# Wide loads for the first three pairs: four tokens a partition, half the heads in each half of the partitions

## The chip, the cores and the metric

The kernel runs on one core of a Trainium2 chip. The metric is the device time of one execution in microseconds (us). Engines are called PE (TensorE, with PEld for its weight loads), DVE (VectorE), ACT (ScalarE), POOL (GpSimd) and SP (SyncE, which here only issues DMAs).

## What is computed

A gated linear attention runs over B = 4 batches, H = 8 heads, S = 768 tokens, D = 48 elements a head. Its output, all heads of a token side by side, goes through a two-layer network with the gate h·cos(h):

```python
for t in range(S):
    state = alpha[:, :, t, :, None] * state + np.einsum('bhd,bhe->bhde', k[:, :, t], v[:, :, t])
    y[:, :, t] = np.einsum('bhd,bhde->bhe', q[:, :, t], state)
x = y.transpose(0, 2, 1, 3).reshape(B * S, H * D)     # [3072, 384]
h = x @ w_in                                          # [3072, 2048]
out = (h * np.cos(h)) @ w_out                         # [3072, 384]
```

alpha, q, k, v lie in DRAM as [4, 8, 768, 48] in fp32, so one token of one head is a run of 192 bytes, and neighbouring tokens of a head are neighbours in memory.

## The kernel before

**Tiling.** The tokens are cut into 12 *pairs* J of 256 tokens, three pairs a batch; each pair has two *chunks* c of 128 tokens, and the state is carried from chunk to chunk. In SBUF a partition holds two neighbouring tokens (e = 0, 1) of all eight heads, so that partitions 0 to 63 are chunk 0 and partitions 64 to 127 chunk 1. `load` (L107 to L121) fills such a tile of 384 KB by one DMA on SP's queue, in runs of two tokens (384 bytes). L110 is that DMA. All loads of a, k, q and v go through SP; W1 (`load_w1`, four pieces u) and W2 (four pieces) are issued by POOL and cast from fp32 to bf16 on the way (L125 to L135).

**One pair** goes through these steps, each a function of its own:

- `ln` (L144, ACT): logarithm of alpha into `lna`. `cums0`/`cums` (L191, L173): cumulative sums of the logarithms over the tokens of a chunk, as matmuls with triangular matrices `tri` and `strict` (L168); pairs 0 to 2 get a sum for each of their two tokens this way, later pairs multiply the two alphas first (`mul_a`, L152, POOL) and subtract (`sub`, L197, DVE). `icp` and `exps` (L206, L213, ACT): exp of minus and of plus that sum; `session` does the four of a later pair and the next pair's `ln`.
- `scale_k`, `scale_q` (L231, L236; DVE or POOL as the plan says): k and q times those exponentials, token by token (e = 0, 1), into `kh` and `qh`.
- `cast_v` (L241, POOL): v to bf16. A second form of v with each chunk's 128 tokens over all partitions comes from `stack_v` (L244, four DMAs on SP) for later pairs, and for pairs 0 to 2 from `stack_v_pe` (L253), four matmuls with a piece of the identity, and `evict_vs` (L261).
- `trans` (L283): transposes of kh and qh by PE, evicted by `evict_T` (L302); the last four pairs use DMA transposes instead (L293).
- `scores` (L308) and `mask` (L317, DVE): k·q of a chunk and the causal mask `msk`. `outer` (L324): the chunk's k outer v into PSUM (L332), `add_state` (L341, DVE) and `decay_state` (POOL) carry the state. `yT` (L358): the pair's output, transposed, evicted by `evict_y` into `xT`.
- The MLP: `mlp1` (four groups u of 512 columns, L401), `cosine` (L408, ACT), `gate` (L413, DVE), `mlp2` (two chunks of four parts, L431), `evict_o` and `store`.

**PSUM** has three buffers of two banks under the tag "h", which transposes, scores, outer products, `stack_v_pe`, `cums0`, `yT` and `mlp1` share, and one bank each under "x" and "o".

**Order.** Nothing is scheduled by itself. `PLAN` (L476 to L545) gives every step of every pair a due number, with an engine for some (":A" is ACT, ":D" DVE). All steps are sorted by number and issued in that order; each engine and each queue then runs its own instructions in the order of issue and waits where data is missing. `IDLE` (L546) puts matmuls of zeros on PE that compute nothing (L458). `GATES` (L99) holds back the loads of pair 3 and of alpha of pair 4 until the last matmul of `mlp2` 0 0 3 has run. On SP the loads stand in the order a1 a0 k0 q0 v0 k1 v1 q1 q2 a2 a3 k2 v2; W1's pieces stand at 380 to 580, W2's at 860 to 1090.

```python
for _, _, kind, args in sorted(order, key=lambda x: x[:2]):
    steps[kind](*args)
```

## Time and profile before

| | |
|---|---|
| median of three runs | 183.82 us (183.24 to 183.96) |
| the profiled execution | 183.31 us, its span 181.5 us |
| PE | 172.4 us busy (95%), 2339 instructions |
| DVE, ACT, POOL | 129.4, 123.9, 82.5 us busy |
| DMA | 31.55 MB, 68840 packets, 59728 of them under 512 bytes |
| SP's and ACT's hardware queue q1 | 27.96 MB, 68.4% of the time of 16 engines |
| POOL's software queue q0 (W1, W2) | 3.15 MB, 11.6% |

The profile's own page gives busy time by engine, then the span in 40 equal slices (of 4.5 us here) in which a digit is the busy share in tenths, PEclk the granted clock, DMA the busy share of the sixteen DMA engines, and GB/s what they moved. Beside it one can list a timeline: each row has the start in us from the span's start, the duration of one instruction, engine, line, operation and tiles, and in brackets the idle time ahead of it with what ended it. A table of stretches gives for chosen windows the length and then busy time (and number of instructions) of PE, PEld, DVE, ACT, POOL, the granted clock, the DMA share and GB/s.

### The profile page before, as it was taken

What the parts mean: (1) busy time and instruction counts of PE and PEld (TensorE: products, weight loads), DVE (VectorE), ACT (ScalarE), POOL (GpSimd) and SP (SyncE); (2) the same over time, 40 slices, a digit from 0 to 9 for tenths busy, and PEclk for the clock granted to TensorE, in tenths of its full rate; (3) what the DMA queues carried; (4) which work ended last, traced back from release to release, by engine and by line L of the source; (5) the groups of instructions that cost most, each with busy time, mean ns of one, the idle gap of its engine ahead of it and who ended that gap; (6) DMA issues with size and microseconds to landing.
All of it is one profiled execution on the core that took longest, in us unless ns stands there. A gap on an engine that the chain in (4) does not pass through costs nothing.

```text
span 181.5 us, 5505 instructions
## 1 busy us (share of the span) xinstructions
PE 172.4 (95%) x2339; PEld 123.6 (68%) x2342; DVE 129.4 (71%) x174; ACT 123.9 (68%) x159; POOL 82.5 (45%) x115
## 2 busy tenths in 40 slices
PE   7898789899999999999999999999999999999993
PEld 2444668665786767866786787778667767766672
DVE  7057976299989779699879898786877873535520
ACT  2765758988798999985688988937497704363201
POOL 6289770437486465959980495409025310000000
PEclk9999999999999999999999999999999999999999
DMA  5999999999969959984994998961669761030222
GB/s 143 261 261 250 153 192 202 247 251 269 236 151 285 263 123 297 276 214 105 298 180 79 269 121 219 185 144 33 131 147 262 89 154 68 2 130 4 87 87 87
DMA packets 68840, 31.55 MB, mean 174 GB/s; under 512 B 59728, under 2 KB 68816, under 8 KB 68816
## 3 DMA queue, kind: packets, MB, share of 16 engines
q1 hardware_dynamic: 64960, 27.96, 68.4%
q0 software_dynamic: 3712, 3.15, 11.6%
q8 instruction: 18, 0.29, 0.7%
q10 hardware_dynamic: 144, 0.10, 0.2%
q14 instruction: 6, 0.05, 0.1%
HBM read 25.17 MB, written 4.72 MB: 165 GB/s over the span
## 4 chain that ended last, share of the span: by engine, by line
PE 70%; DMA 9%; ACT 5%; POOL 4%; SPq 3%; issue 3%; DVE 3%; ACTq 0%
PE o_ps L431 28%; PE h_ps L401 28%; DMA w<-in_moe_w_out_dram 6%; PE y_ps L381 5%; SPq L110 3%; DMA v<-in_v_dram 3%; PE A_ps L314 3%; PE U_ps L332 2%; PE o_last L431 1%; DVE A_sb L320 1%; ACT L141 1%; POOL un L354 1%; POOL w L132 1%; PE T_ps L290 1%; ACT lna L146 1%
## 5 line engine op out<-in xcount | busy, mean ns | idle before, releaser
L413 DVE TENSOR_TENSOR gsb<-h_ps,c_sb 128x1024 bf16<-128x1024 f32 x48 | 57.9, 1222 | 23.0 <-ACT c_sb L408 22.1
L401 PE MATMUL h_ps<-xT,w 128*128 128x256 bf16 x576 | 68.5, 273 | 1.3 <-DVE A_sb L320 0.8
L431 PE MATMUL o_ps<-w,gsb 128*128 128x384 bf16 x368 | 67.0, 326 | 0.8 <-DMA w<-in_moe_w_out_dram 0.8
L408 ACT ACTIVATE c_sb<-h_ps,halfpi 128x1024 bf16<-128x1024 f32 x48 | 52.8, 1114 | 20.8 <-PE h_ps L401 20.6
L401 PEld LDWEIGHTS <-w 128*128 128x128 bf16 x576 | 55.2, 98 | 11.3 <-DMA w<-in_moe_w_in_dram 1.9
L431 PEld LDWEIGHTS <-gsb 128*128 128x128 bf16 x400 | 37.0, 98 | 21.9 <-issue 1.4
L320 DVE TENSOR_TENSOR A_sb<-A_ps,msk 128x1024 bf16<-128x1024 f32 x24 | 29.0, 1218 | 4.4 <-PE A_ps L314 4.2
L354 POOL TENSOR_TENSOR un<-us,c 128x384 bf16<-128x384 f32 x20 | 16.8, 838 | 31.5 <-DVE us L346 24.3
L233 POOL TENSOR_TENSOR kh<-k,icp 128x384 bf16<-128x384 f32 x19 | 19.7, 1038 | 9.1 <-ACT icp L209 5.2
L238 POOL TENSOR_TENSOR qh<-q,cp 128x384 bf16<-128x384 f32 x17 | 17.2, 1024 | 13.0 <-ACT cp L219 10.0
L390 ACT CAST xT<-y_ps 128x384 bf16<-128x384 f32 x12 | 6.7, 594 | 11.4 <-PE y_ps L381 11.3
L444 ACT COPY o_sb<-o_ps 128x384 f32<-128x384 f32 x12 | 5.7, 479 | 11.3 <-PE o_ps L431 11.3
L242 POOL CAST vp<-v 128x768 bf16<-128x768 f32 x12 | 10.1, 845 | 6.0 <-DMA v<-in_v_dram 5.7
L146 ACT ACTIVATE lna<-a 128x768 bf16<-128x768 f32 x12 | 10.1, 843 | 3.2 <-DMA a<-in_alpha_dram 3.2
L458 PE MATMUL idle_ps<-zeros 128*128 128x512 bf16 x38 | 10.8, 426 | 1.5 <-DVE halfpi L77 1.2
L141 ACT ACT_TABLE_LOAD x9 | 11.5, 1283 | 0.9 <-PEq L576 0.7
L408 ACT ACT_TABLE_LOAD x9 | 11.5, 1283 | 0.2
L154 POOL TENSOR_TENSOR a<-a 128x384 f32<-128x384 f32 x9 | 9.0, 1001 | 5.6 <-DMA a<-in_alpha_dram 5.6
L346 DVE TENSOR_TENSOR us<-U_ps,un 128x384 f32<-128x384 f32 x16 | 8.8, 551 | 2.6 <-PE U_ps L332 1.3
L444 DVE COPY o_sb<-o_ps 128x384 f32<-128x384 f32 x11 | 6.1, 555 | 4.8 <-PE o_ps L431 4.7
L314 PE MATMUL A_ps<-qkT 48*128 48x128 bf16 x192 | 8.8, 217 | 0.3 <-issue 0.3
L390 DVE CAST xT<-y_ps 128x384 bf16<-128x384 f32 x12 | 6.6, 586 | 2.1 <-PE y_ps L381 1.9
(68 smaller groups left out, 144.0 us busy)
## 6 DMA issues: line engine op xcount, KB each, us to landing
a<-in_alpha_dram SPq DMA_DIRECT2D x12, 384.0 KB, 5.8
k<-in_k_dram SPq DMA_DIRECT2D x12, 384.0 KB, 5.8
q<-in_q_dram SPq DMA_DIRECT2D x12, 384.0 KB, 6.0
v<-in_v_dram SPq DMA_DIRECT2D x12, 384.0 KB, 5.3
out_dram<-o_sb SPq DMA_DIRECT2D x23, 192.0 KB, 2.2
vs<-vp SPq DMA_DIRECT2D x36, 64.0 KB, 3.1
w<-in_moe_w_in_dram POOLq DMA_DIRECT2D x4, 384.0 KB, 7.0
w<-in_moe_w_out_dram POOLq DMA_DIRECT2D x4, 384.0 KB, 8.6
```

Of the source, the lines that this page charges most:

```text
L141: nc.scalar.preload_act_table_set("natural_log_exp_and_others")
L146: nc.scalar.activation(out=lna_t[J % NL][:, :, :, 0:D].rearrange("p e h d -> p h e d"), in_=a_sb.pop(J), func=AF.Ln)
L233: eng.tensor_tensor(out=kh_t[J % NQ][:, :, e, :, 0:D], in0=kqv["k", J][:, :, e].rearrange("p (n a) d -> p n a d", a=2), in1=icp_.rearrange ...
L238: eng.tensor_tensor(out=qh_t[J % NQ][:, :, e, :, 0:D], in0=kqv["q", J][:, :, e].rearrange("p (n a) d -> p n a d", a=2), in1=cp.rearrange(" ...
L314: last = nc.tensor.matmul(A_ps[J, c][:, a, p, :], qkT[r, c, NP + p, :], qkT[r, c, p, :], start=True, stop=True)
L320: nc.vector.tensor_tensor(out=A_sb[J][:, c].rearrange("s a p t -> s (a p) t"), in0=A_ps.pop((J, c)).rearrange("s a p t -> s (a p) t"), in1 ...
L354: nc.gpsimd.tensor_tensor(out=u, in0=U_sum.pop(n), in1=c2_sb[J][:, :, c].unsqueeze(3).to_broadcast([C, NP, 2, D]), op=ALU.mult)
L390: ins = copy(out=xT[J][:, :, c * C : (c + 1) * C].rearrange("r i (t e) -> r i e t", e=2), in_=y_ps[J][:, c, 0 : KT * C].rearrange("r (i e ...
L401: last = nc.tensor.matmul(h_ps[J, u][:, f, :], w1[:, kk, ft * C : (ft + 1) * C], xT[J][:, kk, :], start=(kk == 0), stop=(kk == KT - 1))
L408: nc.scalar.activation(out=c_sb[J, u], in_=h_ps[J, u], func=AF.Sin, bias=halfpi, scale=1.0)
L413: nc.vector.tensor_tensor(out=gsb[J][:, u * FW : (u + 1) * FW], in0=h_ps.pop((J, u)), in1=c_sb.pop((J, u)), op=ALU.mult)
L431: last = nc.tensor.matmul(o[:, 0 : cols.stop - cols.start], gsb[J][:, ft, c * C : (c + 1) * C], w2[:, ft, cols], start=(done == 1 and ft = ...
```

## The change

Pairs 0, 1 and 2 (`WIDE`) are loaded in another layout. A partition now holds *four* neighbouring tokens (e = 0 to 3) of *four* heads: partitions 0 to 63 hold heads 0 to 3 of all 256 tokens, partitions 64 to 127 heads 4 to 7. A run in memory is 768 bytes, and one load is two DMAs, one for each half of the partitions. Each half in turn is two quarters of 32 partitions, chunk 0 and chunk 1. The steps of these pairs get forms of their own:

- the masks `tri4`, `strict4`, `msk4` are set up by 32-wide copies ahead of the loop (eight on DVE, seven on POOL, after memsets); the masks of the old form (`tri`, `msk`) are filled by a step "later" at due number 1020;
- `sums4` needs seven matmuls for one half of the heads (two heads of each half of the partitions, all four tokens), where the old form needs two for one token of all heads; e in `icp`, `exps`, `scale_k`, `scale_q` now counts halves of the heads instead of tokens;
- `stack_v_pe` takes 16 matmuls into 32 partitions each, and `evict_vs` is split between ACT and DVE; `trans` keeps 32 transposes, all of kh ahead of all of qh, written to interleaved places; `scores` and `yT` keep their matmuls with other views;
- `outer4` does one chunk in 16 matmuls of 32 rows, with a PSUM tile for each chunk (steps "outer 0" and "outer 1"), where `outer` does both chunks in 16 of 64 rows.

The whole plan has new due numbers. On SP the loads now stand in the order a0 v0 a1 k0 q0 v1 k1 q1 a2 k2 q2, and then a4, a3 (held by the gate), v2 and the others; W1's pieces stand at 190 to 540, W2's at 700 to 1070. Idle matmuls go from 41 in the plan (38 of them in the records) to 17. Pairs 3 to 11 keep the form of their steps.

```diff
+    WIDE = (0, 1, 2)
+    QC = C // 4
...
-    for c in range(2):
-        r = slice(HC * c, HC * c + HC)
-        nc.vector.tensor_copy(out=tri[r, c], in_=triu[r, r])
-        nc.vector.tensor_copy(out=strict[r, c], in_=striu[r, r])
-        for e2 in range(2):
-            nc.vector.tensor_copy(out=msk[r, e2], in_=(triu if c <= e2 else striu)[r, r])
+    tri4 = consts.tile([C, C], BF, tag="tri4")
+    nc.gpsimd.memset(tri4, 0.0)
+    strict4 = consts.tile([C, C], BF, tag="strict4")
+    nc.gpsimd.memset(strict4, 0.0)
+    msk4 = consts.tile([C, 4, QC], BF, tag="msk4")
+    inquart = consts.tile([C, 4], BF, tag="inquart")
+    nc.gpsimd.memset(inquart, 0.0)
+    for z in range(4):
+        nc.gpsimd.memset(inquart[QC * z : QC * z + QC, z : z + 1], 1.0)
+
+    def setup_wide():
+        for z in range(4):
+            r = slice(QC * z, QC * z + QC)
+            nc.vector.tensor_copy(out=tri4[r, r], in_=triu[r, r])
+            nc.vector.tensor_copy(out=strict4[r, r], in_=striu[r, r])
+        for z in range(4):
+            r = slice(QC * z, QC * z + QC)
+            if z:
+                nc.gpsimd.tensor_copy(out=msk4[r, 0:z], in_=striu[r, r].unsqueeze(1).to_broadcast([QC, z, QC]))
+            nc.gpsimd.tensor_copy(out=msk4[r, z:4], in_=triu[r, r].unsqueeze(1).to_broadcast([QC, 4 - z, QC]))
+
+    def setup_later(J):
+        for c in range(2):
+            r = slice(HC * c, HC * c + HC)
+            nc.vector.tensor_copy(out=tri[r, c], in_=triu[r, r])
+            if 2 not in WIDE:
+                nc.vector.tensor_copy(out=strict[r, c], in_=striu[r, r])
+            for e2 in range(2):
+                nc.vector.tensor_copy(out=msk[r, e2], in_=(triu if c <= e2 else striu)[r, r])
+
...
+    setup_wide()
...
-        dma = queue.dma_start(
-            out=t.rearrange("p h e d -> p h (e d)"),
-            in_=src[nm][b, :, g * T2 : (g + 1) * T2, :].rearrange("h (p e) d -> p h (e d)", e=2),
-        )
-        if (nm, J) in AFTER:
+        if J in WIDE:
+            dmas = [
+                queue.dma_start(
+                    out=t[HC * x : HC * x + HC].rearrange("s h e d -> s (h e d)").rearrange("s (n f) -> s n f", n=4),
+                    in_=src[nm][b, 4 * x : 4 * x + 4, g * T2 : (g + 1) * T2, :].rearrange("h (s e) d -> s h (e d)", e=4),
+                )
+                for x in range(2)
+            ]
+        else:
+            dmas = [queue.dma_start(
+                out=t.rearrange("p h e d -> p h (e d)"),
+                in_=src[nm][b, :, g * T2 : (g + 1) * T2, :].rearrange("h (p e) d -> p h (e d)", e=2),
+            )]
+        for dma in dmas if (nm, J) in AFTER else []:
...
+    def four(t):
+        return t.rearrange("p (h x) e d -> p h (x e) d", x=2)
+    def by_token(t):
+        return t.rearrange("s e (x h) d -> s (e x) h d", x=2)
     def ln(J):
         act_set("exp")
-        nc.scalar.activation(
-            out=lna_t[J % NL][:, :, :, 0:D].rearrange("p e h d -> p h e d"), in_=a_sb.pop(J), func=AF.Ln
-        )
+        a, l = a_sb.pop(J), lna_t[J % NL]
+        if J in WIDE:
+            a, l = four(a), by_token(l)
+        nc.scalar.activation(out=l[:, :, :, 0:D].rearrange("p e h d -> p h e d"), in_=a, func=AF.Ln)
...
+    def sums4(J, t, x):
+        l = by_token(lna_t[J % NL])
+        o = t[:, 0:HD].rearrange("p (e a d) -> p e a d", e=4, a=2)
+        for i in range(4):
+            for m, lo, hi in ((tri4, i, 4), (strict4, 0, i)):
+                if lo < hi:
+                    r = l[:, i, 2 * x : 2 * x + 2, 0:D].unsqueeze(1).to_broadcast([C, hi - lo, 2, D])
+                    ins = nc.tensor.matmul(o[:, lo:hi], m, r, start=(i == 0), stop=(i == 3), skip_group_check=True)
+                    use(J, x, ins, pe=True)
...
+        if J in WIDE:
+            sums4(J, t, 1)
+            l = by_token(lna)
+            for p in range(2):
+                for e in range(4):
+                    ins = nc.tensor.matmul(t[:, HD : HD + 2 * NP].rearrange("r (x p c) -> r p x c", x=2, p=2)[:, p],
+                                           l[:, e, 2 * p : 2 * p + 2, :].rearrange("s h d -> s (h d)"),
+                                           inquart.rearrange("s (x c) -> s x c", x=2),
+                                           start=(e == 0), stop=(e == 3))
+                    use(J, 1, ins, pe=True)
+            return
...
+    def scale(J, e, eng, nm, to, to4, w):
+        x = kqv[nm, J]
+        if J in WIDE:
+            eng.tensor_tensor(out=to4[J % NQ][:, e, :, :, 0:D], in0=four(x)[:, 2 * e : 2 * e + 2].rearrange("p a e d -> p e a d"),
+                              in1=w.rearrange("p (e a d) -> p e a d", e=4, a=2), op=ALU.mult)
+        else:
+            eng.tensor_tensor(out=to[J % NQ][:, :, e, :, 0:D], in0=x[:, :, e].rearrange("p (n a) d -> p n a d", a=2),
+                              in1=w.rearrange("p (n a d) -> p n a d", n=NP, a=2), op=ALU.mult)
+
     def scale_k(J, e, eng):
-        icp_ = icp_sb.pop((J, e)).rearrange("p (h d) -> p h d", h=H)
-        eng.tensor_tensor(out=kh_t[J % NQ][:, :, e, :, 0:D], in0=kqv["k", J][:, :, e].rearrange("p (n a) d -> p n a d", a=2),
-                          in1=icp_.rearrange("p (n a) d -> p n a d", a=2), op=ALU.mult)
+        scale(J, e, eng, "k", kh_t, kh_4, icp_sb.pop((J, e)))
 
     def scale_q(J, e, eng):
-        cp = cp_sb[J, e][:, 0:HD].rearrange("p (h d) -> p h d", h=H)
-        eng.tensor_tensor(out=qh_t[J % NQ][:, :, e, :, 0:D], in0=kqv["q", J][:, :, e].rearrange("p (n a) d -> p n a d", a=2),
-                          in1=cp.rearrange("p (n a) d -> p n a d", a=2), op=ALU.mult)
+        scale(J, e, eng, "q", qh_t, qh_4, cp_sb[J, e][:, 0:HD])
 
     def cast_v(J):
-        nc.gpsimd.tensor_copy(out=vp_t[J % NV][:, :, :, 0:D].rearrange("s e h d -> s h e d"), in_=kqv.pop(("v", J)))
+        v_, vp = kqv.pop(("v", J)), vp_t[J % NV]
+        if J in WIDE:
+            v_, vp = four(v_), by_token(vp)
+        nc.gpsimd.tensor_copy(out=vp[:, :, :, 0:D].rearrange("s e h d -> s h e d"), in_=v_)
...
+        if J in WIDE:
+            vp = by_token(vp_t[J % NV])
+            for c in range(2):
+                for e in range(4):
+                    for x in range(2):
+                        r, o = slice(HC * x, HC * x + HC), slice(QC * e, QC * e + QC)
+                        nc.tensor.matmul(vs_ps[J][o, x, 4 * D * c : 4 * D * c + 4 * D].rearrange("s (h d) -> s h d", h=4),
+                                         ident_bf[r, HC * x + QC * c : HC * x + QC * c + QC], vp[r, e, :, 0:D],
+                                         start=True, stop=True)
+            return
...
+        vs, t = vs_t[J % NS], vs_ps.pop(J)
+        if J in WIDE:
+            other = copies["ACT" if copy == copies["DVE"] else "DVE"]
+            for x, cp in enumerate((copy, other)):
+                ins = cp(out=vs[:, :, 4 * x : 4 * x + 4, 0:D], in_=t[:, x, 0:HD].rearrange("s (c h d) -> s c h d", c=2, h=4))
+                apart(("vs", J), cp, ins)
+        else:
+            copy(out=vs[:, :, :, 0:D], in_=t[:, :, 0:HD].rearrange("s c (h d) -> s c h d", h=H))
...
+        if J in WIDE:
+            t4 = T_ps[J].rearrange("r x n y s -> r x (n y s)").rearrange("r x (m f) -> r x m f", m=4)
+            for p in range(2):
+                for e in range(4):
+                    for z in range(2):
+                        r = slice(HC * z, HC * z + HC)
+                        nc.tensor.transpose(t4[:, z, 2 + p].rearrange("r (c f) -> r c f", c=2)[:, :, QC * e : QC * e + QC],
+                                            kh_4[J % NQ][r, p, e].rearrange("s a d -> s (a d)"), ident_bf[r, r])
+            for p in range(2):
+                for e in range(4):
+                    for z in range(2):
+                        r = slice(HC * z, HC * z + HC)
+                        nc.tensor.transpose(t4[:, z, p, HC * e : HC * e + HC], qh_4[J % NQ][r, p, e].rearrange("s a d -> s (a d)"),
+                                            ident_bf[r, r])
+            return
...
+    def outer4(J, c):
+        kh, vp = kh_4[J % NQ], by_token(vp_t[J % NV])
+        U_ps[J, c] = two_banks("U_ps")
+        for p in range(2):
+            for e in range(4):
+                for x in range(2):
+                    r = slice(QC * (2 * x + c), QC * (2 * x + c) + QC)
+                    nc.tensor.matmul(
+                        U_ps[J, c][:, x, 2 * p * D : 2 * (p + 1) * D].rearrange("r (a d) -> r a d", a=2),
+                        kh[r, p, e].rearrange("s a d -> s (a d)"),
+                        vp[r, e, 2 * p : 2 * p + 2, 0:D], start=(e == 0), stop=(e == 3))
...
     PLAN = {
-        "load a": "20 10 630 980 1430 1690 1920 2270 2690 2230 3120 4260",
+        "load a": "10 30 670 1200 1110 1410 2050 2400 2710 2610 3380 3770",
-        "load k": "110 240 1160 1450 1740 1900 2300 2840 2330 4130 4240 5280",
+        "load k": "170 470 770 1340 1740 2130 2510 2930 3260 3970 4340 5420",
-        "load q": "140 390 490 1530 1750 2210 2350 2680 3690 3700 4630 5250",
+        "load q": "210 550 910 1360 1650 2040 2380 3000 3450 4110 4480 5080",
-        "load v": "150 340 1200 1560 2180 2470 2660 3190 3380 4570 5030 5440",
+        "load v": "20 390 1290 1530 2180 2120 2490 2820 3590 2740 4770 5940",
-        "w1": "480 380 580 560 - - - - - - - -",
+        "w1": "330 190 540 380 - - - - - - - -",
-        "w2": "1080 1010 1090 860 - - - - - - - -",
+        "w2": "920 830 1070 700 - - - - - - - -",
-        "ln": "50 30 640 1250 - - - - - - - -",
+        "ln": "40 60 680 1280 - - - - - - - -",
-        "cums0": "60 40 870 - - - - - - - - -",
+        "cums0": "70 150 1000 - - - - - - - - -",
-        "cums": "90 160 890 1290 1520 1850 2420 2920 3390 3820 4310 4670",
+        "cums": "100 280 1040 1400 1630 1850 2370 2830 3410 3730 4250 4870",
-        "icp 0": "70 170 900 - - - - - - - - -",
+        "icp 0": "80 260 1140 - - - - - - - - -",
-        "icp 1": "130 210 940 - - - - - - - - -",
+        "icp 1": "110 290 1090 - - - - - - - - -",
-        "exps 0": "80 420 920 - - - - - - - - -",
+        "exps 0": "90 160 1030 - - - - - - - - -",
-        "exps 1": "100 290 910 - - - - - - - - -",
+        "exps 1": "130 350 1180 - - - - - - - - -",
-        "sk 0": "120 250 1190:D 1580 2050 2240 3140 3560 3850 4270 4830 5630",
+        "sk 0": "180:D 480 1150:D 1550:D 1920 2280 2700 3480 3630:D 4380 4660:D 5630",
-        "sk 1": "200:D 460 1170:D 1470:D 2020 2370 2940 3260 3750 4230 4990 5550:D",
+        "sk 1": "200:D 520 1100:D 1560:D 1930 2220 3110 3540 3800 4420 4800:D 5640",
-        "sq 0": "220:D 430:D 1110 1540:D 1970 2220 2640 3330 3960 4640 4780 5510:D",
+        "sq 0": "230:D 570:D 1130 1580:D 1670 2150 2660:D 3400 3910 4320 4960:D 5450:D",
-        "sq 1": "180 400:D 1150 1550:D 2040 2290:D 2780 3400 3990 4620 5150 5570",
+        "sq 1": "220:D 560:D 1190 1590:D 1980 2100 3090 3550 3620 4120 4940 5520:D",
-        "castv": "190 350 1300 1650 2190 2770 3050 3920 4340 4740 5090 5790",
+        "castv": "50 400 1310 1540 2190 2140 2680 3240 3740 4590 4780 5950",
-        "vpe": "450 410 1410 - - - - - - - - -",
+        "vpe": "120 410 1510 - - - - - - - - -",
-        "vev": "470:A 440:A 1500:A - - - - - - - - -",
+        "vev": "140:A 420:A 1520:A - - - - - - - - -",
-        "trans": "230 500 1270 1590 2060 2590 3170 3580 - - - -",
+        "trans": "270 580 1240 1600 2000 2600 3120 3560 - - - -",
-        "evT 0": "260:A 530:A 1330 1600:A 2140:A 2620 3250 3600 - - - -",
+        "evT 0": "320 590 1330:A 1610:A 2210 2630 3130:A 3580 - - - -",
-        "evT 1": "310:A 520 1350 1640 2070 2670 3280 3590 - - - -",
+        "evT 1": "300 610:A 1250 1730 2080 2620 3140 3570 - - - -",
-        "scores 1": "320 680 1360 1670 2310 3440 3420 3800 4410 4800 5400 5850",
+        "scores 1": "310 650 1680 1820 2250 3370 3270 3950 4510 4980 5390 5810",
-        "outer": "360 650 1310 1660 2540 3080 3150 3940 4360 4760 5370 5800",
+        "outer": "- - - 1790 2570 3160 3150 3900 4160 4600 5270 5960",
-        "m2 0 3": "970 1510 2460 3000 3490 4420 5010 5450 5930 6180 6350 6590",
+        "m2 0 3": "1010 1700 2800 3300 3850 4680 5180 5560 5850 6220 6420 6610",
+        "outer 0": "240 530 1440 - - - - - - - - -",
+        "outer 1": "440 740 - - - - - - - - - -",
+        "later": "1020 - - - - - - - - - - -",
-    IDLE = [(35, 10), (55, 3), (225, 9), (265, 5), (315, 6), (405, 4), (495, 3), (605, 1)]
+    IDLE = [(65, 8), (235, 1), (405, 4), (485, 1), (595, 3)]
```

More of the change, by code (lines that the diff above doesn't have):

```diff
@@ L313, in scores @@
                 r = slice(64 * a, 64 * a + D)
+                if J in WIDE:
+                    kT, qT = wide_qkT(J)
+                    last = nc.tensor.matmul(A_ps[J, c][:, a, p, :].rearrange("s (e t) -> s e t", e=4),
+                                            kT[r, c, p // 2, p % 2], qT[r, c, p // 2, :, p % 2], start=True, stop=True)
+                    continue
                 last = nc.tensor.matmul(A_ps[J, c][:, a, p, :], qkT[r, c, NP + p, :], qkT[r, c, p, :], start=True, stop=True)
```

47 lines of the change are left out of this document (33 added, 14 removed), and 84 rows, old and new, of the table PLAN.

## The prediction

> **What bounds the kernel now.** I read the page's slices first, then the stretches of 5 us, then the timeline of the first 40 us.
>
> ```profile
> PE   7898789899999999999999999999999999999993
> PEclk9999999999999999999999999999999999999999
> DMA  5999999999969959984994998961669761030222
> GB/s 143 261 261 250 153 192 202 247 251 269 236 151 285 263 123 297 276 214 105 298 180 79 269 121 219 185 144 33 131 147 262 89 154 68 2 130 4 87 87 87
> ```
>
> The reader sees an array that is full from the eleventh slice on at an undisturbed clock, and transfers that are full for the first ten. Two regimes follow. Until the first MLP matmul the kernel waits for inputs and for the chain of pairs 0 and 1; behind it TensorE is the bound.
>
> ```profile
> 4.53 0.84 ACT L146 ACTIVATE lna<-a 128x768 bf16<-128x768 f32 x1 [2.51 <-DMA a<-in_alpha_dram]
> 6.04 0.84 ACT L146 ACTIVATE lna<-a 128x768 bf16<-128x768 f32 x1 [0.66 <-DMA a<-in_alpha_dram]
> ...
> 13.59 0.82 POOL L242 CAST vp<-v 128x768 bf16<-128x768 f32 x1 [0.25 <-DMA v<-in_v_dram]
> ...
> 14.35 0.93 POOL L126 DMA_DIRECT2D w<-in_moe_w_in_dram  x1
> ...
> 16.32 1.02 DVE L238 TENSOR_TENSOR qh<-q,cp 128x384 bf16<-128x384 f32 x2
> ...
> 17.85 1.01 ACT L305 COPY qkT<-T_ps 128x1024 bf16<-128x1024 bf16 x1
> ...
> 21.14 1.03 PE L401 MATMUL h_ps<-xT,w 128*128 128x256 bf16 x8 [0.75 <-DVE A_sb L320]
> ```
>
> This is the timeline's start: one load lands every 1.51 us (4.53, 6.04; the seventh at 13.59 = 4.53 + 6 x 1.51), so load n lands at 3.02 + 1.51n. W1 is asked for only at 14.35, behind the loads that pairs 0 and 1 need. The first MLP matmul runs at 21.14. From there the last matmul ends at 178.4; the 5-us stretches show 2.6 us of idle PE in all of it, none after 70 us. The profiled execution took 183.31 us: span 181.5 and 1.8 around it. The median of the three runs is 183.82, so I sum against 183.31 and add 0.5 at the end.
>
> **The price of a wide load.** Bytes stay 384 KB; packets double to 768 bytes, but one transfer now writes 64 partitions, and two follow each other. No row shows this pair of properties. The nearest, as stretches (last two columns DMA share and GB/s):
>
> ```profile
> 6.00:14.00 8.00, 7.20 (x84) 3.63 (x83) 2.85 (x3) 5.79 (x11) 5.05 (x6) 1.00 1.28 261
> 82.10:82.58 0.48, 0.48 (x28) 0.41 (x20) 0.48 (x2) 0.48 (x2) 0.47 (x1) 1.00 0.61 137
> 158.95:159.95 1.00, 1.00 (x9) 0.59 (x7) 0.00 (x0) 1.00 (x1) 0.00 (x0) 1.00 0.99 363
> ```
>
> The first is today's loads: 393 thousand bytes at 261 GB/s are 1.51 us. The third is two stores of 1536-byte rows from 128 partitions, 363 GB/s: a load at that pace takes 1.08 us, the lower end. The second is one stack copy of L248, 64 KB into 64 partitions with nothing beside it, 137 GB/s although its runs are 1 KB: 2.87 us, the upper end, start and stop included. I take 1.65 us: the stack copy is the only row that writes half the partitions, so I go to the slow side of today's 1.51; I stay near it because queued loads have no start and stop between them.
>
> [...]
>
> **Start, step by step.** New order on SP: a0 v0 a1 k0 q0 v1 k1 q1 a2, two issues each; landing n at 3.02 + 1.65n. On POOL the first three W1 pieces now stand directly behind the cast of v0 (13.59 to 14.35 becomes about 7 us: v0 lands second at 6.3, cast 0.85). A W1 piece is 384 KB at 198 GB/s (stretch 26 to 32 us), 2.0 us. So q1, eighth in both orders, gets W1 in front of it: none at all up to three pieces, by what stands in the queues first; I take two. q1 lands at 3.02 + 8 x 1.65 + 2 x 2.0 = 20.2 us (now 15.1). Then: both q scales on DVE 1.02, transposes and their latency 0.45 (17.40 to 17.85), eviction on ACT 1.01, the two scores of pair 1, which stand ahead of the first MLP matmul on PE, 0.40. The first MLP matmul comes at 23.1, **1.95 later** than 21.14.
>
> Hidden here: the logs wait on ACT (the log of pair 1 now stands ahead of all exponentials of pair 0, which wait with it for a1, the third load: 8.0 against q1's 20.2); the cumulative sums in fourteen matmuls instead of four (twice the columns; +0.65 a pair, cover: q1 is not there); eight 32-wide mask copies on DVE against eight wider ones, and on POOL seven more copies and seven memsets (0.1 to 0.2 each, about 2 us behind 3.45) that end near v0's landing; the half evictions of the stack on ACT and DVE. Without q1's wait this chain gives 18.4 at 1.1 us a load: a1 6.3, log 0.84, four exponentials 0.42 apart 8.9, scales 10.1, transposes 10.6, two evictions on DVE 11.9, two masks 14.4, half eviction, sum and pair 1's q scales 16.4, transposes 16.9, eviction 17.9, scores 18.4. Idle matmuls fall from 38 to 17; ten of them at the start take 3.80 us, nine later 2.10, so a cold array could add; zero to 1.5 us, I take zero (the granted clock reads 1.00 in every stretch).
>
> **Behind the first MLP matmul.**
> - More TensorE work: pair 2's sums +0.65 (four 384-column matmuls 0.16 apart today), the second chunk of pair 1's outer products +0.45 (L332 x16 in the chain), pair 2's own +0.1, its sixteen small stack matmuls +0.2 (four take 0.36 now; from 0 to twice): **+1.4**.
> - Idle that goes: W1 and W2 asked for earlier. Now PE waits 0.43 at 27.2 for W1 and:
>
> ```profile
> 36.17 0.81 PE L431 MATMUL o_ps<-w,gsb 128*128 128x384 bf16 x4 [0.79 <-DMA w<-in_moe_w_out_dram]
> ```
>
>   With 0.3 of gaps between the first MLP groups: **-1.5**. Next late after W2 is the gate of pair 3's loads, which opens with the same output matmul as before.
> - Idle that comes: pair 3.
>
> ```profile
> 41.65 0.32 PE L168 MATMUL cums<-lna,tri 128*128 128x384 bf16 x1
> ...
> 46.22 0.41 PE L290 MATMUL T_ps<-ident_bf,kh 64*128 64x64 bf16 x16
> ```
>
>   From its sums to its transposes pass 4.6 us, a chain of subtraction, exponentials and four scales (0.5 each on DVE), under which PE has outer products, scores and four output groups. The new order leaves under it outer products 0.45, one score 0.33, two output groups 1.3 and the stack 0.5: 2.6. On DVE the new half eviction of pair 2's stack stands ahead of pair 3's scales, and all four scales now run there. Idle is 0 to 2.0; I take **+1.5**.
> - Six mask copies ("later", 1.1 us on DVE) lie in DVE's 4.16 us wait at 31 to 35: nothing. Without that wait, 1.1.
> - Pairs 3 to 11 keep their forms and get a new order. PE is full there with or without it: nothing, within 1 either way.
>
> Sum: +1.95 + 1.4 - 1.5 + 1.5 = +3.35, so 186.7 on the profiled execution's scale, **187.2** on that of the median: 1.8% slower.
>
> **Rivals.**
> 1. *Full pace.* The 768-byte packets run at the stores' pace, 1.1 us a load, one W1 piece ahead of q1: q1 lands at 3.02 + 8.8 + 2.0 = 13.8 and no longer decides; the compute chain gives 18.4, 2.7 early. Sum -2.7 + 1.4 - 1.5 + 1.5 = -1.3: 182.5, faster. For it: 363 GB/s with long rows. Against it: 137 into half the partitions. It decides below about 1.25 us a load, where the start comes before 19.7. Chance 0.28.
> 2. *No change of pace.* The halves cost what the longer packets give: 1.5 us a load. With one piece ahead q1 lands at 17.0 and the start is 19.9 (184.0), with two 21.9 (186.0): 185.0. For it: every load of this trace runs at that rate. Chance 0.20.
> 3. [...] Chance 0.07.
>
> The forecast keeps 0.45. The range 181.5 to 190.0 takes in rivals 1 and 2 with the idle of pair 3 at either end, and leaves out rival 3 and the tails. About 0.5% (0.9 us) is what a measurement can tell from no change. Faster than that: most of rival 1, 0.26; within it: the ends of rivals 1 and 2, 0.12; slower: 0.62.
>
> **What would show it.** In the profile after: the GB/s of 4 to 8 us, before any W1, above 300 for rival 1, near 260 for rival 2, near 240 for the forecast, under 210 for rival 3; the start of pair 1's q scales on DVE (20.2, and whether it waits for q's DMA); the first MLP matmul (23.1); idle PE before pair 3's transposes (1.5); W2's wait gone. I would be wrong most cheaply through the pace of a load: each 0.1 us of it moves q1, and so the end, by 0.8. I would also be wrong if W1 does not pass in front of q1 at all (4 us less), or if the new order fills pair 3's gap.

## The result and the profile after

The changed kernel takes **198.23 us** in the median of four runs (196.44 to 200.95), the kernel before 183.53: a ratio of **1.071** (95% interval 1.066 to 1.076). The forecast was 187.2, range 181.5 to 190.0: the direction was right, the loss four times as large. Two of the four runs, at 199.85 and 200.95 us, had a lower granted clock (0.956 and 0.940 against 0.974) and are left out of the ratio. The profiled execution took 196.61 us (span 194.7) against 183.31, 13.3 more.

The page's slices of the changed kernel (4.9 us each):

```profile
PE   7769269899958999999999999999999999999993
PEclk9997958999999999999999999999999999999999
DMA  4999992999976992979895798537577463303112
GB/s 128 241 220 234 250 185 49 129 157 285 249 205 149 238 270 56 275 195 282 220 247 144 163 203 156 117 107 141 94 188 191 60 153 100 116 3 117 45 43 81
```

Three things are new: a hole in PE in the fifth slice, a granted clock below full in the slices around it, and a second dip of PE in the twelfth. The timeline from 5 to 32 us shows what the first hole waits for:

```profile
7.71 2.48 POOL L165 DMA_DIRECT2D w<-in_moe_w_in_dram  x3
...
21.45 1.95 POOL L305 TENSOR_TENSOR kh<-k,icp 128x384 bf16<-128x384 f32 x2 [3.73 <-DMA k<-in_k_dram]
...
23.83 1.97 DVE L305 TENSOR_TENSOR qh<-q,cp 128x384 bf16<-128x384 f32 x2 [4.36 <-DMA q<-in_q_dram]
...
25.86 0.61 PE L392 MATMUL T_ps<-ident_bf,qh 64*128 64x64 bf16 x16 [1.72 <-DVE qh L305]
...
26.50 1.01 ACT L415 COPY qkT<-T_ps 128x1024 bf16<-128x1024 bf16 x1 [4.92 <-PE T_ps L392]
...
27.79 1.03 PE L432 MATMUL A_ps<-qkT 48*128 48x128 bf16 x16
...
28.76 2.54 PE L545 MATMUL h_ps<-xT,w 128*128 128x256 bf16 x12
```

W1's three pieces are asked for at 7.71 us; k and q of pair 1, the seventh and eighth loads, land behind them at 21.45 and 23.83. The first MLP matmul comes at 28.76, **7.6 later** than the 21.14 of before, and its twelve matmuls take 2.54 us where the same twelve took 1.47. The stretches (length; PE, PEld, DVE, ACT, POOL; clock; DMA share; GB/s) tell why:

```profile
12.00:14.00 2.00, 0.76 (x33) 0.59 (x31) 1.51 (x4) 0.00 (x0) 0.00 (x0) 0.97 1.18 224
14.00:18.00 4.00, 3.67 (x50) 2.40 (x50) 3.09 (x4) 0.88 (x2) 1.83 (x3) 0.59 1.19 233
18.00:24.00 6.00, 2.55 (x109) 1.76 (x93) 1.64 (x4) 2.34 (x3) 2.55 (x3) 1.00 1.13 243
24.00:30.00 6.00, 3.95 (x50) 2.41 (x44) 4.51 (x6) 3.04 (x3) 3.19 (x5) 0.51 1.15 191
```

Twice the array stands idle (0.76 busy of 2, 2.55 of 6), and in the stretch behind it its clock is about half (0.59 and 0.51). A cold array or a cold clock means this half clock below. Not every idle stretch brings it: before_w1_early shows one below. The twelfth slice is pair 3's chain on DVE:

```profile
52.87 1.81 DVE L308 TENSOR_TENSOR kh<-k,icp 128x384 bf16<-128x384 f32 x2
53.08 1.19 POOL L201 TENSOR_TENSOR a<-a 128x384 f32<-128x384 f32 x1 [1.89 <-DMA a<-in_alpha_dram]
53.48 0.20 PE L400 MATMUL T_ps<-ident_bf,kh 64*128 64x64 bf16 x2 [0.40 <-DVE kh L308]
...
54.61 1.67 DVE L308 TENSOR_TENSOR qh<-q,cp 128x384 bf16<-128x384 f32 x2
54.74 0.38 PE L400 MATMUL T_ps<-ident_bf,kh 64*128 64x64 bf16 x14 [1.06 <-DVE kh L308]
...
56.33 0.38 PE L400 MATMUL T_ps<-ident_bf,qh 64*128 64x64 bf16 x14 [0.90 <-DVE qh L308]
```

PE waits three times, 2.4 us in all, for four scales that take 0.8 to 0.9 us each in the mean of a pair (0.55 to 1.35 us singly), with POOL working beside them.

The account of the 13.3: the start, +7.6; PE's work behind it, 158.2 against 155.4 us busy, +2.8 (1.1 of it the cold twelve matmuls); idle PE behind the start, 4.55 against 1.93, +2.6; the rest, 0.3, is rounding and the ends.

### The profile page after: what moved, and what is told of

It is laid out like the page before. It is cut to its first block, busy times and chain, and to the rows that moved or that the text cites. A ratio compares the mean times of both kernels' runs of the same rounds, so it can differ in the third digit from the quotient of the medians.

```text
span 194.7 us, 5728 instructions
## 1 busy us (share of the span) xinstructions
PE 176.8 (91%) x2421; PEld 127.5 (66%) x2424; DVE 140.1 (72%) x192; ACT 122.8 (63%) x157; POOL 78.4 (40%) x122
## 4 chain that ended last, share of the span: by engine, by line
PE 78%; DMA 7%; DVE 5%; SPq 5%; ACT 2%; issue 1%; DVEq 0%
PE h_ps L545 33%; PE o_ps L575 31%; DMA q<-in_q_dram 7%; SPq L142 5%; PE y_ps L525 4%; PE A_ps L435 2%; PE U_ps L453 2%; PE o_last L575 1%; PE T_ps L400 1%; DVE qh L305 1%; DVE xT L534 1%; DVE kh L308 1%; ACT xT L534 1%; DVE qh L308 1%; PE cums_h L219 1%
## 5 line engine op out<-in xcount | busy, mean ns | idle before, releaser
L552 ACT ACTIVATE c_sb<-h_ps,halfpi 128x1024 bf16<-128x1024 f32 x48 | 52.7, 1114 | 23.6 <-PE h_ps L545 23.2
L545 PEld LDWEIGHTS <-w 128*128 128x128 bf16 x576 | 56.0, 99 | 11.1 <-issue 1.8
L492 POOL TENSOR_TENSOR un<-us,c 128x384 bf16<-128x384 f32 x20 | 17.7, 887 | 34.1 <-DVE us L483 32.2
L308 POOL TENSOR_TENSOR qh<-q,cp 128x384 bf16<-128x384 f32 x12 | 12.0, 1004 | 8.8 <-ACT cp L290 5.5
L588 ACT COPY o_sb<-o_ps 128x384 f32<-128x384 f32 x15 | 7.2, 478 | 11.8 <-PE o_ps L575 11.7
L308 POOL TENSOR_TENSOR kh<-k,icp 128x384 bf16<-128x384 f32 x13 | 12.8, 1003 | 4.2 <-DMA k<-in_k_dram 4.2
L588 DVE COPY o_sb<-o_ps 128x384 f32<-128x384 f32 x8 | 4.4, 554 | 10.7 <-PE o_ps L575 8.3
L534 DVE CAST xT<-y_ps 128x384 bf16<-128x384 f32 x16 | 9.5, 641 | 2.8 <-PE y_ps L525 2.8
L201 POOL TENSOR_TENSOR a<-a 128x384 f32<-128x384 f32 x9 | 9.1, 1020 | 4.9 <-DMA v<-in_v_dram 2.5
L534 ACT CAST xT<-y_ps 128x384 bf16<-128x384 f32 x8 | 6.0, 831 | 5.0 <-PE y_ps L525 5.0
L415 ACT COPY qkT<-T_ps 128x1024 bf16<-128x1024 bf16 x4 | 4.0, 1008 | 7.8 <-PE T_ps L392 4.9
L415 DVE COPY qkT<-T_ps 128x1024 bf16<-128x1024 bf16 x12 | 8.0, 684 | 0.9 <-PE T_ps L392 0.7
```

The source lines that it names most:

```text
L308: eng.tensor_tensor(out=to[J % NQ][:, :, e, :, 0:D], in0=x[:, :, e].rearrange("p (n a) d -> p n a d", a=2), in1=w.rearrange("p (n a d) -> ...
L415: ins = copy(out=qkT_sb[J][:, c], in_=T_ps[J][:, c].rearrange("r n e s -> r n (e s)"))
L492: nc.gpsimd.tensor_tensor(out=u, in0=U_sum.pop(n), in1=c2_sb[J][:, :, c].unsqueeze(3).to_broadcast([C, NP, 2, D]), op=ALU.mult)
L534: ins = copy(out=xT[J][:, :, c * C : (c + 1) * C].rearrange("r i (t e) -> r i e t", e=ne), in_=y_ps[J][:, c, 0 : KT * C].rearrange("r (i e ...
L545: last = nc.tensor.matmul(h_ps[J, u][:, f, :], w1[:, kk, ft * C : (ft + 1) * C], xT[J][:, kk, :], start=(kk == 0), stop=(kk == KT - 1))
L552: nc.scalar.activation(out=c_sb[J, u], in_=h_ps[J, u], func=AF.Sin, bias=halfpi, scale=1.0)
```

## Experiments

Ratios are to the kernel before on the same chip, with 95% intervals; "start" is the first MLP matmul in the run's trace, which is of one execution and not of the median. The two wide_128 runs load other tokens and heads than the computation needs, as many bytes, and so show time alone.

| run | median us | ratio | start |
|---|---|---|---|
| changed kernel | 198.23 | 1.071 (1.066 to 1.076) | 28.76 |
| w1_behind_v1 | 193.15 | 1.051 (1.044 to 1.059) | 24.61 |
| w1_behind_k1 | 194.04 | 1.055 (1.048 to 1.063) | 24.61 |
| more_idle | 195.56 | 1.070 (1.061 to 1.079) | 26.41 |
| before_w1_early | 187.42 | 1.021 (1.016 to 1.026) | 21.32 |
| wide_old_order | 188.08 | 1.025 (1.019 to 1.030) | 23.88 |
| narrow_new_order | 193.04 | 1.053 (1.046 to 1.059) | 26.72 |
| before_half_loads | 188.41 | 1.025 (1.021 to 1.030) | 25.45 |
| wide_128_partitions | 192.03 | 1.043 (1.035 to 1.050) | 22.80 |
| new_order_mended | 192.33 | 1.048 (1.045 to 1.051) | 24.37 |
| narrow_mended | 186.35 | 1.015 (1.010 to 1.021) | 22.21 |
| before_new_load_order | 185.83 | 1.013 (1.011 to 1.016) | 22.19 |
| wide_128_old_order | 187.27 | 1.024 (1.019 to 1.030) | 22.00 |
| before_aligned | 184.17 | 1.002 (1.000 to 1.004) | 21.32 |
| mended_pair3 | 191.61 | 1.042 (1.038 to 1.047) | 24.05 |
| mended_aligned | 192.49 | 1.048 (1.044 to 1.052) | 24.69 |
| narrow_pair3_aligned | 186.98 | 1.014 (1.010 to 1.018) | 21.50 |
| mended_pair3_busy | 191.44 | 1.041 (1.038 to 1.044) | 24.29 |
| before_17_idle | 185.27 | 1.008 (1.006 to 1.009) | 22.25 |

### Does W1's early place cost it, and the cold clock?

```diff
 w1_behind_v1
-        "w1": "330 190 540 380 - ..."
+        "w1": "403 402 540 404 - ..."
 w1_behind_k1
+        "w1": "523 522 540 524 - ..."
 more_idle
-    IDLE = [(65, 8), (235, 1), (405, 4), (485, 1), (595, 3)]
+    IDLE = [(65, 8), (235, 1), (265, 5), (405, 4), (485, 1), (525, 12), (575, 7), (595, 3)]
 before_w1_early (the kernel before)
-        "w1": "480 380 580 560 - ..."
+        "w1": "193 192 580 194 - ..."
```

> The changed kernel with only the due numbers of three W1 pieces moved from 190, 330 and 380 to 402, 403 and 404, behind the cast of v1 on POOL. Theory 1 (three W1 pieces, asked for at 7.7 us, take the DMA engines in front of k1 and q1, which is most of the loss): q1 lands near 16 to 17 us instead of 23.8, the first MLP matmul comes at 20 to 21.5 instead of 28.76, and the time is 186.5 to 189. Rival (the loads into half the partitions, or the new forms of the steps, cost it): the first MLP matmul stays above 25 and the time above 193.

> The same with the three W1 pieces at 522, 523 and 524, behind the two k scales of pair 1 on POOL, so that hardly any of W1 can stand in front of q1. Theory 1: q1 at 16 to 16.5, but W1 now late: first MLP matmul at 20 to 21 with waits for W1 behind it, 187 to 189. Rival: above 193.

> The changed kernel with 24 more idle matmuls of zeros on PE (5 ahead of pair 0's transposes, 12 ahead of pair 1's first outer products, 7 ahead of pair 1's transposes), nothing else changed. If the granted clock, which is 0.50 from 24.5 to 30 us, falls because the array stands idle, it stays near 1.00 up to the first MLP groups, q1 lands where it did (23.8) and 1.5 to 2.5 us go: 194 to 195. If idle time does not set the clock: 196 to 197.

> The kernel before, narrow loads and all, with only three W1 pieces moved to stand directly behind the cast of v0 on POOL (due numbers 192 to 194). Theory 1: W1 is asked for near 11.6 instead of 14.35 to 18.3, q1 lands near 19 to 21 instead of 15.1, the first MLP matmul moves from 21.14 to 24.5 to 27, and the time is 187 to 190. Rival (W1 ahead costs little, the wide form costs it): within 1 us of 183.5.

Moving W1 takes 4.2 us off the start and about 2 points off the ratio. By the DMA records of w1_behind_v1's trace q1 now lands at 16.79, as expected, 6.9 us earlier than in the changed kernel. But the time falls to 193.15 where 186.5 to 189 was expected, and the start, 24.61, lies between what the theory and what its rival gave. No wait for k or q of pair 1 is left:

```profile
17.85 1.95 POOL L305 TENSOR_TENSOR kh<-k,icp 128x384 bf16<-128x384 f32 x2
19.65 2.20 DVE L305 TENSOR_TENSOR qh<-q,cp 128x384 bf16<-128x384 f32 x2
...
24.61 1.48 PE L545 MATMUL h_ps<-xT,w 128*128 128x256 bf16 x12 [0.79 <-DMA w<-in_moe_w_in_dram]
```

The steps themselves are the next limit (at a clock of 0.50 from 14 to 18 us), with W1 itself late at the end: its first piece lands at 24.56. With more idle matmuls the profiled execution held its clock (0.99 to 1.00 from 14 to 30 us, where the changed kernel fell to 0.59 and 0.51; it was 0.72 from 10 to 16) and the start came 2.35 earlier, 1.1 of it because q1 came earlier (22.72 against 23.83). But the four runs spread from 192.4 to 197.1 and the ratio cannot be told from the changed kernel's. In the kernel before, an early W1 costs 2.1%, the time that was expected, but by another way: q1 was already in, the start stayed at 21.32, and it is the third alpha that comes late (ACT waits 4.9 us for it, and PE 2.9 behind that). The array is then idle for most of 26 to 30 us, and its clock stays at 1.00 behind it:

```profile
26.00:28.00 2.00, 0.61 (x6) 0.39 (x4) 0.00 (x0) 1.99 (x2) 0.47 (x1) 1.00 1.30 197
28.00:30.00 2.00, 0.51 (x5) 0.46 (x5) 1.79 (x2) 2.00 (x3) 0.00 (x0) 1.00 1.31 203
30.00:35.00 5.00, 5.00 (x49) 4.10 (x48) 2.92 (x3) 4.16 (x7) 0.23 (x1) 1.00 0.81 127
```

### Forms or order? A two by two

wide_old_order is the changed kernel with the old PLAN and IDLE; narrow_new_order is its plan with narrow loads and old forms:

```diff
 wide_old_order (old PLAN and IDLE, and)
+        "outer 0": "360 650 1310 - ...",
+        "outer 1": "549 709 - ...",
+        "later": "1020 - ...",
 narrow_new_order
-    WIDE = (0, 1, 2)
+    WIDE = ()
-    setup_wide()
+    setup_later(0)
-        "outer": lambda J, c=None: outer(J) if c is None else outer4(J, c)
+        "outer": lambda J, c=0: outer(J) if c == 0 else None
```

> The wide loads and their own forms of the steps, but the plan and the idle matmuls of the kernel before (outer 0 at outer's old numbers, outer 1 just ahead of add 1). This is the forms without the new order. Theory 1, as amended by the first four runs (the new order with W1 early, and the array going idle and cold, cost more than the wide forms): q1 lands at 17 to 18 us, two above the kernel before, the first MLP matmul at 22.5 to 24, and the time is 186 to 188.5. Rival (the wide forms are what costs it): above 191.

> The plan and the 17 idle matmuls of the changed kernel, but narrow loads and the old forms of all steps (outer 0 stands for the whole of outer, outer 1 and later do nothing, the old masks are set up ahead of the loop). Theory 1: W1 still goes ahead of k1 and q1, the gap of pair 3 (2.4 us) stays and the clock falls; 189 to 193. Rival (the wide forms cost it): 183 to 186.

The forms alone cost 2.5%, the order alone 5.3%, both 7.1%. **Two thirds of the loss or more is the new order** with its 17 idle matmuls: 5.3 points with narrow loads, 4.6 with wide ones (7.1 less 2.5). The clock of narrow_new_order was 0.50 in the trace from 10 to 16 and from 20 to 30 us.

### What does writing half of the partitions cost?

```diff
 before_half_loads, for J in (0, 1, 2): x in range(2)
+    out=t[HC * x : HC * x + HC].rearrange("p h e d -> p h (e d)"),
+    in_=src[nm][b, :, g * T2 + C * x : g * T2 + C * x + C, :].rearrange("h (p e) d -> p h (e d)", e=2),
 wide_128_partitions, wide_128_old_order
+    out=t.rearrange("p h e d -> p (h e d)").rearrange("p (n f) -> p n f", n=4),
+    in_=src[nm][b, 0:4, first : first + 2 * T2, :].rearrange("h (s e) d -> s h (e d)", e=4),
```

> The kernel before with each load of pairs 0 to 2 in two DMAs, one for partitions 0 to 63 and one for 64 to 127, runs of 384 bytes as before; everything else unchanged. If writing half of the partitions at a time is slower, GB/s from 6 to 14 us falls from 261 to 225 to 240, q1 lands 1 to 2.5 us later and the time is 184 to 186. If halves cost nothing: 261 GB/s and 183 to 183.7.

> The changed kernel, but each wide load is one DMA into all 128 partitions, runs of 768 bytes, of four heads of 512 tokens: as many bytes and packets, other data than the reference asks for. Everything else, W1's early place included, stays. If the half partitions hold the 768-byte packets back, GB/s from 6 to 10 us rises from 230 to above 300, and k1 and q1 land 2 to 4 us earlier: 192 to 195. If they do not: 225 to 270 GB/s and within 1.5 us of the changed kernel.

> The wide forms with the plan of the kernel before (as in wide_old_order, 188.1), but each wide load in one DMA into all 128 partitions, runs of 768 bytes, of four heads of 512 tokens: the bytes and packets of the wide load, other data than the reference asks for. If the half partitions are what keeps 768-byte packets from paying, GB/s from 6 to 14 us is above 300 instead of 222, the first MLP matmul comes at 20 to 21.5 instead of 23.9, and the time is 184 to 185.5. If the steps' own forms cost it: 187 or more.

The stretch from 6 to 14 us in before_half_loads, then wide_old_order, then wide_128_old_order:

```profile
6.00:14.00 8.00, 6.13 (x72) 3.22 (x72) 1.12 (x2) 4.33 (x9) 3.15 (x3) 1.00 1.30 203
```

```profile
6.00:14.00 8.00, 7.71 (x100) 4.74 (x99) 1.83 (x2) 4.63 (x10) 3.01 (x3) 1.00 1.11 222
```

```profile
6.00:14.00 8.00, 7.76 (x98) 4.66 (x98) 1.84 (x3) 4.90 (x11) 5.07 (x6) 1.00 1.04 324
```

Runs of 384 bytes moved at 261 GB/s into all partitions (the kernel before) and at 203 into halves, runs of 768 bytes at 324 and at 222. Whether the 324 against 261 is the longer run is not shown: the tiles also lie at other places in SBUF, and a better place alone gives the short runs as much (below). In the old order the faster loads change the time by nothing that can be told (1.0244 against 1.0248), although the start in the trace came 1.9 us earlier. So the forms' 2.5% is not mainly the loads. In the new order it is another matter: wide_128_partitions starts at 22.80 instead of 28.76 and costs 4.3% instead of 7.1%. Behind W1's three pieces the pace of the loads did count (337 GB/s from 6 to 10 us against 231).

### Can the order be mended?

```diff
 new_order_mended, narrow_mended
+        "w1": "403 402 540 404 - ..."
-        "m2 0 0": "1120 1750 ..."     "m2 0 3": "1010 1700 ..."
+        "m2 0 0": "1120 1598 ..."     "m2 0 3": "1010 1596 ..."
+    IDLE = [(65, 11), (235, 3), (265, 5), (405, 4), (485, 2), (575, 4), (595, 3)]
 mended_pair3 (new_order_mended, and)
-        "sk 0": "180:D 480 1150:D 1550:D ..."   "mula": "- - - 1210 1350 1430 ..."
+        "sk 0": "180:D 480 1150:D 1550 ..."     "mula": "- - - 1210 1350 1555 ..."
+            other = copies["ACT" if J == 2 or copy == copies["DVE"] else "DVE"]
 mended_pair3_busy (new_order_mended, and in trans)
+        for i, x in ([(1, kh_t[J % NQ])] + [(0, kh_t[J % NQ])] * (4 if J == 3 else 0) + [(0, qh_t[J % NQ])]):
 before_17_idle (the kernel before)
+    IDLE = [(35, 8), (225, 1), (405, 4), (495, 1), (605, 3)]
```

> The changed kernel, wide forms and all, with what the first runs hold against its order mended: three W1 pieces behind the cast of v1 (402 to 404), 32 idle matmuls instead of 17, all ahead of the first MLP matmul, and two of pair 1's output groups (m2 0 0 and m2 0 3) moved from behind pair 3's transposes to just ahead of them, where the array stood idle. If W1's early place, the cold clock and pair 3's gap are what the order costs, little more than the wide forms' own cost (4.1 us in the old order) is left: 187 to 189.5, first MLP matmul at 22.5 to 24, granted clock 0.99 or more. If something else of the order costs it: above 191.

> The same mended order with narrow loads and the old forms of all steps. Narrow loads in this order ran at 306 to 325 GB/s in the run before, against 261 in the kernel before. If that rate holds, q1 lands near 13 us and the first MLP matmul comes at 20 to 21.5: 183 to 186. If the order itself is bad beyond W1, clock and gap: above 188.

> new_order_mended (192.3) with three steps changed around pair 3: its first k scale on POOL as in the kernel before, the multiplication of alpha of pair 5 behind it, and both halves of pair 2's stack evicted by ACT. If the crowding of DVE is the cause of pair 3's gap (2.7 us of idle array from 45 to 55 us there, and a granted clock of 0.6 to 0.7 behind it), the gap shrinks by 1 to 2 us, the clock holds and the time is 189 to 190.5. If the gap is set by something else: 191.5 to 192.5.

> new_order_mended (192.3, ratio 1.048) with 64 more transposes between pair 3's transposes of kh and of qh, which write kh where qh's transposes are written after them, and so change nothing of the result; they lie in waits for DVE's q scales. If the cold clock behind the gap is what costs, it is 0.9 or more from 50 to 60 us instead of 0.60 to 0.71 and 1.5 to 2.5 us go (190 to 191). If the waits themselves are all of it: 192 to 193.

> The kernel before with the idle matmuls cut to the changed kernel's 17 (8, 1, 4, 1 and 3, at the old due numbers 35, 225, 405, 495 and 605); nothing else. If the array goes cold without them in the old order too: granted clock 0.5 to 0.9 somewhere between 10 and 25 us and 184.5 to 187. If the old order's own work keeps it warm: 1.00 and 183.0 to 184.

With narrow loads the three repairs together take the order from 5.3% to 1.5%: W1's place, the cold array and pair 3's gap are most of what it costs. With wide loads 4.8% is left, 192.33 us where 187 to 189.5 was expected, so there something else costs too. Giving pair 3's first scale to POOL mostly moved the wait (PE now waits 1.63 us for POOL's kh; 2.5 us idle from 45 to 55 instead of 2.7) and won 0.6 points, within the intervals. With the array kept busy in those waits the clock held. The stretch from 50 to 60 us, first in new_order_mended, then in mended_pair3_busy:

```profile
50.00:60.00 10.00, 7.54 (x137) 5.81 (x138) 8.55 (x11) 6.67 (x10) 4.81 (x6) 0.66 0.77 200
```

```profile
50.00:60.00 10.00, 7.60 (x219) 6.24 (x212) 8.56 (x12) 7.67 (x11) 6.68 (x8) 1.00 0.69 176
```

The clock is 0.66 in the first and 1.00 in the second, and 0.7 points went (1.048 to 1.041): the cold clock there is worth about 1.3 us. Executions of one kernel say the same: in mended_pair3 the two with a clock of 0.991 over the whole span took 190.63 and 190.93 us, the two at 0.982 took 192.29 and 192.65.

The kernel before paid no such price. There the cut to 17 idle matmuls alone costs 0.8%, but not by the clock: the profiled execution was at 0.50 from 8 to 16 us, started at 22.25 and took 183.60, no longer than the kernel before, while the four others, at 1.00, took 185.24 to 185.75. In its trace the start is 1.1 later and PE idles 0.8 less behind it, because W1 and W2 have come in by then. What makes the four others longer is open.

### Why did narrow loads run faster in the new kernel?

In narrow_mended they ran at 286 GB/s from 6 to 14 us, against 261 in the kernel before. The order of the loads or the place of their tiles in SBUF could do it: the new masks move the tiles.

```diff
 before_new_load_order (the kernel before: a0 v0 a1 k0 q0 v1 k1 q1 a2 k2 q2 first)
+        "load a": "10 12 640 ..."   "load k": "13 240 650 ..."
+        "load q": "14 390 660 ..."  "load v": "11 235 1200 ..."
+        "ln": "30 50 645 ..."       "cums0": "40 60 870 ..."
 before_aligned (the kernel before)
+    pad = consts.tile([C, 144], BF, tag="pad")
+        if nm == "k" and not kqv:
+            gap = sb.tile([C, 208], BF, tag="gap", name="gap", bufs=1)
 mended_aligned, narrow_pair3_aligned: the gap alone (and pair 3's step as above)
```

> The kernel before with only SP's first loads in the changed kernel's order (a0 v0 a1 k0 q0 v1 k1 q1 a2 k2 q2 instead of a1 a0 k0 q0 v0 k1 v1 q1 q2 a2), with the log and first sums of pair 0 ahead of those of pair 1 to suit. If the order of the loads is what lifted narrow loads from 261 to 306 GB/s, GB/s from 4 to 12 us is above 295, q1 lands near 13 instead of 15.1 and the time is 181.5 to 183; if not, 261 GB/s and 183 to 185.

> The kernel before with two unused tiles (288 bytes a partition among the constants, 416 ahead of the first k tile) that move every load tile of a, k, q and v to a multiple of 512 bytes in its partition; nothing else. If the place of the tiles in SBUF sets the pace of 384-byte runs: GB/s from 4 to 14 us rises from 261 to 300 to 325, q1 lands near 13 instead of 15.1 us, the first MLP matmul comes at 19.5 to 20.5 instead of 21.14, and the time is 182 to 183 (the chain of the steps takes over). If the place is nothing: 261 GB/s and 183.0 to 183.9.

> new_order_mended with one unused tile of 416 bytes that moves the k and q tiles to a multiple of 512 bytes, as a and v are already. If the place counts for half loads too, GB/s from 8 to 16 us rises from 223 to 242 to 265 or more and the time falls by 0.5 to 1.5 us (191 to 192); if the half partitions set the pace, 223 to 245 GB/s and 192 to 192.6.

> narrow_mended (186.35) with both: the k and q tiles moved to a multiple of 512 bytes, and pair 3's first k scale on POOL with the multiplication of pair 5 behind it. If both theories hold: 300 GB/s and more up to 13 us instead of 275 to 287, pair 3's gap (1.8 us) halved, 183.5 to 185.5. If neither: 186 to 187.

before_new_load_order stays at 261 to 262 GB/s in every stretch from 4 to 16 us: it is not the order. before_aligned, 6 to 14 us, and its start:

```profile
6.00:14.00 8.00, 7.28 (x84) 3.71 (x83) 2.93 (x3) 4.67 (x10) 4.91 (x6) 1.00 1.17 325
```

```profile
15.28 1.01 POOL L238 TENSOR_TENSOR kh<-k,icp 128x384 bf16<-128x384 f32 x1
16.77 1.03 DVE L243 TENSOR_TENSOR qh<-q,cp 128x384 bf16<-128x384 f32 x2
...
21.32 1.47 PE L406 MATMUL h_ps<-xT,w 128*128 128x256 bf16 x12 [0.75 <-DVE A_sb L325]
```

Moving the tiles to multiples of 512 bytes lifted the same loads from 261 to 325 GB/s, and **the time does not fall**: q1 lands at 12.61 instead of 15.04 by the DMA records, but pair 1's scales and the start come nearly where they came (16.32 and 21.14 before). The loads were not what the start waited for. In the new order narrow_pair3_aligned has 325 GB/s from 6 to 14 us too, against narrow_mended's 286, and does not gain either (186.98 against 186.35 us). For half loads the place counted less: 252 GB/s from 8 to 16 us in mended_aligned against 229 in new_order_mended, and 192.49 against 192.33 us: no gain there either. No version tried beats the kernel before.

## Why the prediction was wrong, step by step

The sum was 186.7 on the profiled execution's scale, the result 196.61: 9.9 short. The start was 5.7 short (28.76 against 23.1), the work behind it 1.4, the idle behind it 2.6.

- **The step that failed: "none at all up to three pieces ... I take two", and with it a q1 that lands at 20.2.** All three pieces went ahead: by the trace's DMA records they landed at 16.06, 19.54 and 22.62, and q1 behind them at 23.71; its scale starts at 23.83. Worked out with the trace's numbers: first load at 5.34, 1.70 a load (393 KB at 231 GB/s from 6 to 10 us), three pieces of 2.0: 3.64 + 8 x 1.70 + 6.0 = 23.2. The third piece is 2.0 of the 3.6 us that q1 came later than forecast; the later first load (0.6) and the pace (0.4) are smaller, and 0.6 is not accounted for.
- **The price of a wide load** was right: 1.65 forecast, 1.70 from 6 to 10 us. It was a choice between distant rows, and in part luck: 324 GB/s into all partitions and 222 into halves lie on either side of the 261 of before. For half of the partitions the traces give 203 GB/s (384-byte runs, before_half_loads, 6 to 14 us), 222 (768-byte runs, wide_old_order, 6 to 14) and 252 (768-byte runs, mended_aligned, 8 to 16).
- **The premise, that q1 sets the start in the kernel before too,** failed: before_aligned has q1 in 2.4 us earlier and starts at 21.32. The forecast's own rows could have told: q1 at 15.1 and 2.9 behind it give a start of 18.0, not 21.14, and the row of q's scale at 16.32 shows no wait for a DMA. The 21.14 was a balance: slower loads cost at once (before_half_loads, start 25.45, +2.5%), faster ones win nothing. The trace of before_half_loads has a clock of 0.51 from 22 to 28 us, but its execution with the highest clock, 0.997, took as long as the others (188.45), so the clock is not shown to be part of it. Rival 1, full pace, did not win its 2.7 us where that pace was run: wide_128_old_order (324 GB/s from 6 to 14 us) starts at 22.00, wide_128_partitions (337 from 6 to 10) at 22.80.
- **From q1 to the start** I took 2.9; it was 4.93: the two scales 1.97 instead of 1.02 (POOL works beside them), transposes to eviction 0.70 instead of 0.45, a wait of 0.28 for the sum of the state, scores to the first MLP matmul 0.97 at half clock instead of 0.40, and the eviction 1.01 as taken.
- **"a cold array could add; zero to 1.5 us, I take zero"** failed at the value taken. The clock was 0.51 from 24 to 30 us. I read "the granted clock reads 1.00 in every stretch" as a property of the kernel; with 17 of the idle matmuls the same order fell to 0.50 from 8 to 16 us (before_17_idle).
- **Behind the start:** +1.4 of work was nearly right (1.7 without the cold twelve). The waits for W1 and W2 went as forecast; waits for xT came in their place (0.66 and 0.63). Pair 3's idle was taken at 1.5 and measured at 2.4, above the bound of 2.0: "all four scales now run" on DVE was read right and priced at 0.5 each, and they take 0.8 to 0.9.
- **Rivals.** Rival 3 (chance 0.07) was to show in less than 210 GB/s from 4 to 8 us. No run shows wide loads that slow: the changed kernel moved 254 GB/s there and 231 from 6 to 10 us, 1.70 us a load, wide_old_order 222 from 6 to 14. None of the rivals put the loss where most of it is, in the order.

What stays open: why the wide forms lose the 3.3 points that divide new_order_mended from narrow_mended. The two traces show where: the start holds 2.2 us (24.37 against 22.21), PE's work behind it 3.4 (158.9 against 155.6 us busy, the cold stretch at pair 3 in it with about 1.3) and idle PE 0.9. In the old order wide_old_order's trace, against that of the kernel before, has 2.7 at the start (23.88 against 21.14), 1.3 of work (156.8 against 155.4, at full clock) and 1.6 of idle PE. Which step of the wide forms makes the start later was not tried by itself; the pace of the loads is not enough, as wide_128_old_order starts 1.9 earlier and is no faster that can be told.

## What to carry to other kernels

Before pricing a faster transfer, make today's transfer faster and slower by itself: a start in balance lost at once when the loads slowed and won nothing when they sped up (25.45 us at 203 GB/s and 21.32 at 325, against 21.14 at 261). When an order is rewritten, follow each request for a large late transfer to what it is now issued behind; here three weight pieces, asked for at 14 to 18 us before, moved to 8 and passed two loads that the start needs. An idle stretch of the array can be paid twice, as wait and as a lower clock behind it (here a clock of 0.66 from 50 to 60 us, about 1.3 us at pair 3; 0.50 from 8 to 16 us and no loss by it in before_17_idle, where PE waited anyway), so fillers and their number are part of the order.

## What the hardware showed that was not expected

- **The place of the tiles changed the pace of the 384-byte runs.** Into tiles that lie 224 (a) or 320 bytes (k, q, v) beyond a multiple of 512 they ran at 261 GB/s, at multiples of 512 at 325. One more place was run, in narrow_mended (a and v at multiples of 512, k and q 96 bytes beyond): 286 from 6 to 14 us. What in the place does it is not shown.
- **DVE beside POOL.** The scale of 128x384 takes 0.55 us on DVE alone and up to 1.35 with POOL at work, least, median and most in ns in the changed kernel:

```profile
L308 DVE TENSOR_TENSOR qh<-q,cp x6: 549/670/1183, 54.6 to 148.4; 128x384 bf16<-128x384 f32 x6
L308 DVE TENSOR_TENSOR kh<-k,icp x5: 548/548/1349, 52.9 to 129.8; 128x384 bf16<-128x384 f32 x5
```

  In the traces of the kernel before, the changed kernel and mended_pair3 each of these scales that ran without POOL took 0.54 to 0.56 us. Beside POOL some took as little and some twice as long and more; what decides it was not tried.
